# Gated feed-forward of six batches in pairs by seven block products instead of eight

## The chip, the cores and the metric

The kernel runs on one core of one Trainium2 chip. The metric is the device time of one launch in microseconds (us). Before the change three runs took 706.78, 707.29 and 708.10 us; their median is 707.29 us. The profile is one more execution, which took 706.64 us, of which 704.8 us lie between its first and its last instruction (its span).

## What is computed

Attention of 8 batches and 8 heads whose queries are pooled in twos (1152 keys, 576 pooled queries, 64 values a head), and then a feed-forward layer with a capacity: a gate scores the 576 rows of each batch, the 128 best go through two layers, and their rows are updated. All of it is float32.

```python
q_pool = q.reshape(B, H, S // 2, 2, D).mean(axis=3)
attn   = softmax(q_pool @ k.T / sqrt(D)); x = attn @ v            # (B, 576, 512) when the heads are put side by side
scores = x @ w_gate
for b in range(B):
    top = argpartition(-scores[b], 128)[:128]
    h   = maximum(x[b, top] @ w1, 0)                              # w1 512 x 1024
    ye  = h @ w2                                                  # w2 1024 x 512
    out[b, top] = x[b, top] + sigmoid(scores[b, top])[:, None] * ye
```

## The kernel before

The instructions of each engine are in the order in which the Python code records them (`manual_schedule`), and every engine works through its own list in that order. An engine waits where an operand isn't ready.

**Halves.** The work is cut by batch and pair of heads (32 pairs), and each pair into two halves of 288 pooled queries. `run` (L1307) goes through 64 halves, h = 0 to 63, four pairs and so eight halves to a batch. In the text S(h) is the start of the scores of half h on TensorE. One turn of the loop records, in this order:

- `scores(h)` (L807): nine times four matmuls into a PSUM tile of two banks, each emptied by a ScalarE exponential (`p`, L825);
- small ScalarE work for the sums: in even halves `side_by_side` (`groups`, L887), in odd ones `spread` (`sums`, L902), which reads `total`;
- `units(mid=True)`: pieces of the routing and of the feed-forward that are marked "mid";
- `gated(h-3)`, `folded(h)` (POOL adds p blocks to `acc`, L857; VectorE reduces `p` and `acc` to `fold`, L862, and then `sum`, L872), `multiplied(h-2)` (`prod`, POOL, L925), and in even halves `prepare_pair` (POOL `qp`, VectorE `kT` and `qT`);
- `weighted(h-1)` (L827): 36 matmuls with the values, the ScalarE copy `two` (L844) and the POOL addition `av` (L846); then `drained(h-1)` (VectorE `avb`, L915);
- in even halves `added` (VectorE `total`, L893), in odd ones `normalized` (VectorE `rec`, L954, and POOL `x`, L956);
- `units(mid=False)`: the pieces that are not marked "mid".

So on TensorE the mid pieces of half h stand between the scores of h and the weighting of h-1; on ScalarE they stand ahead of `two` of h-1, and so ahead of the exponentials of h+1; on VectorE the pieces at the end of h stand behind `avb` of h-1 and `total`, ahead of `folded(h+1)`.

**PSUM.** All TensorE results go through one pool, `psum`, of four tiles of two banks (`banks`, L994), used in turn. The fourth tile of `scores(h+2)` is the one that `weighted(h)` filled, and is free when `two` has copied it.

**Routing.** When a batch's gate scores are there, `routed` (L997) is a generator. Its pieces rank the rows (VectorE, L1083 to L1102), broadcast rank and gate through DRAM (`row_rank`, `lines`), pick out the 128 rows (`pick`, VectorE, L1166), make the row index (POOL, L1175), fetch the rows with an indirect DMA (POOL, L1183), transpose them (L1197), and do the first layer (L1208, 32 matmuls of 128x128 by 128) and the second (L1221, 8 of 128x128 by 512). The first layer of a batch is one mid piece, the second another. The second layer of batch 5 and both layers of batches 6 and 7 come behind the loop, where `pieces` calls in `run` interleave them by hand with the ranking of the last batch.

**The end.** The last batch's route is a chain: `acc`, `prod`, `av`, `x` on POOL; `red`, `part`, `line`, `diag` on VectorE; L1054 on TensorE; ranks on VectorE from L1092 to `pick` L1143; L1152 on TensorE; the index copied by ScalarE (L1159); the fetch by POOL (L1183); transposes (L1197); two layers; L1230; the write.

**Transfers.** Keys, queries and values of a pair come by SP's DMA queue: `load_pair` records keys and queries of pair n+2 in the second half of pair n, and `load_values` there too. Buffers: keys 2, queries 2, values 3.

## Time and profile before

| what | value |
|---|---|
| profiled execution, device time | 706.64 us |
| its span | 704.8 us |
| TensorE busy | 694.4 us (99%) |
| VectorE, ScalarE, POOL busy | 496.5, 444.5, 485.1 us |
| scores, L818 | 295.2 us |
| weighting, L836 | 294.6 us |
| first layers, L1208 | 59.3 us |
| second layers, L1221 | 57.3 us |
| DMA | 82.86 MB, 118 GB/s mean |

In the groups of the profile each line is: source line, engine, operation, written tile <- read tiles, shapes, count; then busy time, mean duration of one in ns, and idle time of the engine ahead of it with what ended it. The timeline's columns are start, length, engine, line, operation, tiles, shape and count, and in brackets idle time just before it with what ended it. A float32 matmul shows as two TensorE records, so 32 matmuls are "x64".

### The profile page before, as it was taken

The page shows a single profiled execution, that of the slowest core. Times are in us where ns is not written, and L with a number is a line of the kernel's source. Part 1 is how long each engine was busy: PE and PEld are TensorE (multiplying, and loading weights), DVE is VectorE, ACT ScalarE, POOL GpSimd, SP SyncE. Part 2 cuts the span into 40 slices and gives each one's busy share as a digit, 9 for nine tenths or more (in the row PEclk, how much of TensorE's full clock was granted, in tenths as well). Part 3 has the DMA queues.
Part 4 walks back from the last instruction along what each step waited for, and adds up shares of the span by engine and source line. Part 5 has one row for each costly group of instructions (what it writes and reads, how often), then busy time and mean ns, then how long its engine had stood idle before and what let it go on. Part 6 is the DMA issues. An engine that isn't in the chain of part 4 may idle for free.

```text
span 704.8 us, 23397 instructions
## 1 busy us (share of the span) xinstructions
PE 694.4 (99%) x9948; PEld 516.8 (73%) x9948; DVE 496.5 (70%) x793; ACT 444.5 (63%) x963; POOL 485.1 (69%) x452
## 2 busy tenths in 40 slices
PE   8999999999999999999999999999999999999996
PEld 5668899996758866688656887578775787766573
DVE  3877777996559965498754988559774697689540
ACT  6677778777547775477746776467754777477210
POOL 5877777868658695586955779467874877686520
PEclk9999999999999999999999999999999999999999
DMA  8888887858486483756928468382775728432200
GB/s 175 172 178 180 171 166 137 146 116 161 85 149 111 85 162 75 145 97 111 172 40 159 81 129 160 66 148 61 161 130 85 135 56 169 83 72 62 45 31 35
DMA packets 389490, 82.86 MB, mean 118 GB/s; under 512 B 376640, under 2 KB 376640, under 8 KB 389376
## 3 DMA queue, kind: packets, MB, share of 16 engines
q1 hardware_dynamic: 387872, 76.49, 58.1%
q0 software_dynamic: 1280, 4.20, 1.8%
q8 instruction: 80, 1.31, 0.8%
q10 hardware_dynamic: 224, 0.59, 0.3%
q14 instruction: 34, 0.28, 0.1%
HBM read 69.65 MB, written 11.59 MB: 115 GB/s over the span
## 4 chain that ended last, share of the span: by engine, by line
PE 89%; POOL 5%; issue 2%; DMA 1%; ACT 1%; DVE 1%; SPq 0%; POOLq 0%; DVEq 0%; ACTq 0%
PE ps L836 36%; PE ps L818 36%; PE ps L1208 8%; PE ps L1221 7%; POOL acc L857 2%; ACT p L825 1%; DMA kb<-in_k_dram 1%; DMA xe<-out_dram,index 1%; PE ps L1197 1%; POOL prod L925 1%; POOL x L956 0%; POOL av L846 0%; DVE fold L862 0%; POOL index L1175 0%; SPq L759 0%
## 5 line engine op out<-in xcount | busy, mean ns | idle before, releaser
L825 ACT ACTIVATE p<-ps 128x576 f32<-128x576 f32 x576 | 320.2, 695 | 1.7 <-PE ps L818 1.3
L818 PE MATMUL ps<-qT,kT 64*64 64x288 f32 x4608 | 295.2, 404 | 0.2 <-ACT p L825 0.2
L836 PE MATMUL ps<-p,v_sb 64*64 64x288 f32 x4608 | 294.6, 403 | 0.0
L857 POOL TENSOR_TENSOR acc<-p 128x576 f32<-128x576 f32 x192 | 266.3, 1417 | 15.4 <-ACT p L825 15.1
L836 PEld LDWEIGHTS ps<-p,v_sb 64*64 64x64 f32 x4608 | 215.5, 133 | 65.3 <-ACT p L825 9.2
L818 PEld LDWEIGHTS ps<-qT,kT 64*64 64x64 f32 x4608 | 208.0, 132 | 73.0 <-ACT p L825 15.4
L862 DVE TRANSPOSE_TENSOR_REDUCE fold<-p 128x54 f32<-128x1728 f32 x64 | 126.0, 1969 | 50.2 <-ACT p L825 50.2
L862 DVE TRANSPOSE_TENSOR_REDUCE fold<-acc 128x54 f32<-128x1728 f32 x64 | 125.3, 1957 | 46.0 <-POOL acc L857 45.8
L844 ACT COPY two<-ps 128x576 f32<-128x576 f32 x64 | 40.9, 639 | 156.9 <-PE ps L836 143.8
L846 POOL TENSOR_TENSOR av<-two 128x288 f32<-128x288 f32 x64 | 51.2, 800 | 96.5 <-ACT two L844 94.9
L915 DVE STREAM_TRANSPOSE avb<-av 128x288 f32<-128x288 f32 x64 | 29.4, 460 | 66.5 <-POOL av L846 66.5
L956 POOL TENSOR_TENSOR x<-avb,rec 128x576 f32<-128x576 f32 x32 | 37.1, 1159 | 40.3 <-DVE rec L954 27.9
L1208 PEld LDWEIGHTS ps<-xeT,w 128*128 128x128 f32 x512 | 57.8, 192 | 2.7 <-ACT p L825 2.6
L1208 PE MATMUL ps<-xeT,w 128*128 128x128 f32 x512 | 59.3, 277 | 0.0
L1221 PE MATMUL ps<-w,hT 128*128 128x512 f32 x128 | 57.3, 598 | 0.0
L925 POOL TENSOR_TENSOR prod<-avb,w_gate 128x288 f32<-128x288 f32 x64 | 51.5, 805 | 0.6 <-DVE avb L915 0.6
L902 ACT ACTIVATE sums<-total,tiny 32x18 f32<-32x18 f32 x124 | 38.1, 308 | 15.9 <-DVE total L893 14.2
L732 POOL TENSOR_TENSOR qp<-qb 128x576 f32<-128x576 f32 x31 | 43.8, 1414 | 2.2 <-DMA qb<-in_q_dram 2.2
L1221 PEld LDWEIGHTS ps<-w,hT 128*128 128x128 f32 x128 | 23.6, 190 | 28.1 <-issue 25.8
L735 DVE STREAM_TRANSPOSE kT<-kb 128x1152 f32<-128x1152 f32 x31 | 42.5, 1370 | 0.0
L887 ACT COPY groups<-sum 32x36 f32<-32x36 f32 x124 | 27.1, 219 | 6.7 <-DVE sum L872 5.2
L981 DVE TENSOR_TENSOR part<-red,rec 128x18 f32<-128x18 f32 x32 | 27.0, 845 | 1.1
(95 smaller groups left out, 290.6 us busy)
## 6 DMA issues: line engine op xcount, KB each, us to landing
kb<-in_k_dram SPq DMA_DIRECT2D x124, 144.0 KB
qb<-in_q_dram SPq DMA_DIRECT2D x124, 144.0 KB
v_sb<-in_v_dram SPq DMA_DIRECT2D x124, 144.0 KB
out_dram<-x SPq DMA_DIRECT2D x128, 72.0 KB
lines<-row_rank SPq DMA_DIRECT2D x7, 640.0 KB
w<-in_moe_w_dram SPq DMA_DIRECT2D x8, 512.0 KB
sc_row<-row SPq DMA_DIRECT2D x7, 288.0 KB
acc<-in_q_dram ACTq DMA_DIRECT2D x2, 288.0 KB
```

The costliest lines, as they stand in the source:

```text
L732: nc.gpsimd.tensor_tensor(out=qp[:, :, :], in0=pair["q"][:, :, 0, :], in1=pair["q"][:, :, 1, :], op=ALU.add)
L735: nc.vector.transpose(kT.rearrange("p (c g i) -> p c g i", c=self.NC, i=BLK), pair["k"].rearrange("p (g c) d -> p c g d", c=self.NC),)
L818: nc.tensor.matmul(sc[keys, j, 0:n], lhsT=pair["kT"][rows, c * P + keys.start : c * P + keys.stop], rhs=pair["qT"][rows, qs], start=True, ...
L825: nc.scalar.activation(p[:, c // G, c % G, :, :], sc[:, :, 0:n], AF.Exp, scale=self.scale)
L836: nc.tensor.matmul(av[j * self.D : (j + 1) * self.D, e, 0:n], lhsT=half["pair"]["v"][keys, j, c, :], rhs=half["p"][keys, c // G, c % G, j, :],
L844: nc.scalar.copy(two[:, :, :], av[:, :, 0:n])
L846: nc.gpsimd.tensor_tensor(out=half["av"][:, :], in0=two[:, 0, :], in1=two[:, 1, :], op=ALU.add)
L857: nc.gpsimd.tensor_tensor(out=acc[:, u, :], in0=units[:, 0, u, :], in1=units[:, 1, u, :], op=ALU.add)
L862: nc.vector.tensor_reduce(fold[:, a, :], of.rearrange("p u (m d) -> p (u m) d", d=BLK), AX.X, ALU.add, apply_transpose=True,)
L925: self.nc.gpsimd.tensor_tensor(out=pair["prod"][:, ns, :], in0=pair["avb"][:, ns, :], in1=self.w_gate[:, hp : hp + 1, :].broadcast_to([P, ...
L1208: nc.tensor.matmul(pv[:, f, 0:w], lhsT=self.w1[:, c, (f0 + f) * P : (f0 + f + 1) * P], rhs=xeT[:, c, 0:w], start=(c == 0), stop=(c == self ...
L1221: nc.tensor.matmul(ps[0:w, 0 : self.Dm], lhsT=hT[:, f, 0:w], rhs=self.w2[:, f, :], start=(f == 0), stop=(f == self.NFC - 1),)
```

## The change

Batches 0 and 1, 2 and 3, 4 and 5 go through the feed-forward as pairs. Their 256 rows and the weights are each cut into two by two blocks, and a layer is done by seven block products and 15 block sums (Strassen's scheme in Winograd's form) instead of eight products. In the first layer a product is 8 matmuls of 128x128 by 128, in the second 4 of 128x128 by 256. Batches 6 and 7 stay as they are (`layers`).

```diff
+    def weight_sums(self):
+        ...
+        for layer in (2, 1):
+            ...
+            for i, (to, x, y) in enumerate(((t1, b12, b11), (t2, b22, t1), (t3, b22, b12), (t4, b21, t2))):
+                nc.vector.tensor_tensor(out=to, in0=x, in1=y, op=ALU.subtract)      # 128x1024, L718
+                nc.sync.dma_start(kept[:, i, :], self.tw[:, i, :])                  # L719
+                yield
+    def load_sums(self, layer):
+        for i in range(0, 4, 2):
+            self.nc.sync.dma_start(self.tw[:, i : i + 2, :], self.tw_kept[layer][:, i : i + 2, :])   # L724
+            yield
+    def input_sums(self, a, s):
+        ...
+        for i, (to, x, y, op) in enumerate(
+            ((s1, a21, a22, add), (s2, s1, a11, subtract), (s3, a11, a21, subtract), (s4, a12, s2, subtract))
+        ):
+            self.nc.gpsimd.tensor_tensor(out=to, in0=x, in1=y, op=op)               # L1321
+            if i % 2:
+                yield i == 3
+    def seven_products(self, layer, a, s, c, rest, shape):
+        ...
+        steps = (
+            (a11, b11, c11, ()),
+            (s1, t1, c22, ()),
+            (s3, t3, c21, ()),
+            (s2, t2, u, ((u, c11), (c21, u), (u, c22), (c22, c21))),
+            (s4, b22, c12, ((c12, u),)),
+            (a12, b21, x, ((c11, x),)),
+            (a22, t4, y, ((c21, y),)),
+        )
+        copies = []
+        for i, (of, by, to, _) in enumerate(steps):
+            if i % 2 == 0:
+                tile = self.banks()
+            ...
+                    nc.tensor.matmul(                                               # L1355
+                        args[0], lhsT=args[1], rhs=args[2], start=k == 0, stop=k == n - 1
+                    )
+            ...
+            if i % 2 or last:
+                for copy in copies:
+                    nc.scalar.copy(*copy)                                           # L1363
+                copies = []
+            yield last
+        for *_, sums in steps:
+            for to, of in sums:
+                nc.vector.tensor_tensor(out=to, in0=to, in1=of, op=ALU.add)         # L1368
+    def layers_of_two(self, tokens):
+        ...
+        yield from self.seven_products(1, a, s, c, rest, lines)
+        loads = self.load_sums(2)
+        next(loads)
+        yield "mid"
+        for i, tile in enumerate(hidden):
+            nc.scalar.activation(tile[:, :, 0:w], tile[:, :, 0:w], AF.Relu)         # 128x1024, L1395
+            yield True if i else "mid"
+        for _ in loads:
+            pass
+        room, s = self.room_of_sums(self.NFC // 2, w)
+        for last in self.input_sums(c, s):
+            yield "hidden" if last else True
+        ...
+        yield from self.seven_products(2, quarters(hidden, self.NFC // 2), s, c, rest, lambda bank: bank[0:w, 0:half])
+        yield "mid"
+        for i, of in enumerate(c):
+            nc.scalar.activation(of, of, AF.Copy, scale=tokens[i // 2]["gate"][0:w, 0:1])   # 128x256, L1411
+        yield True
+        for i, of in enumerate(c):
+            ...
+            nc.gpsimd.tensor_tensor(out=to, in0=of, in1=to, op=ALU.add)             # 128x256, L1416
+            if i % 2:
+                self.written(token)
+                yield True
+        if tokens[1]["b"] + 1 < self.paired:
+            for _ in self.load_sums(1):
+                yield True
-                nc.gpsimd.tensor_scalar(
+                nc.vector.tensor_scalar(
                     out=index[0:w, :],
...
+                if b < self.B - 2:
+
+                    yield True
...
-        qb = self.load.tile([P, self.QB, 2, BLK], F32, name="qb")
+        qb = self.load.tile([P, self.QB, 2, BLK], F32, name="qb", bufs=1)
-        v_sb = pair["v"] = self.load.tile([P, 2, self.NC, self.D], F32, name="v_sb", bufs=3)
+        v_sb = pair["v"] = self.load.tile([P, 2, self.NC, self.D], F32, name="v_sb", bufs=2)
...
-                        self.load_values(loaded)
+                    if n + 1 < len(pairs):
+                        self.load_values(upcoming)
...
+                if h > 10 and s == 1:
+                    next(sums, None)
```

Other edits make room: several small tiles get fewer buffers (`prod` 1, `fold`, `groups`, `line` 2), `cmp`, `tie`, `flags` share the tile `pick`, the last batch's `diag` and fetched rows share `lines`, the first pair is loaded into a `p` tile, and `slot_f` is gone (`token_line` is used for it). The `pieces` calls behind the loop have other counts.

**Where it stands in the engines' lists** (from the built program; line numbers of the changed kernel):

- TensorE: the seven first-layer products of a pair are one block of 56 matmuls, between the scores of half 28 and the weighting of half 27 (and again at 44 and 60). The seven second-layer products are a block of 28 matmuls in halves 32 and 48; those of the third pair stand behind the loop. Behind the loop TensorE has: transposes of batch 6, the `sum` matmul (L967), products 1 to 3, the `diag` matmul (L1083), product 4, the `sc_row` columns (L679), products 5 to 7, 12 of the 32 first-layer matmuls of batch 6, the `pick` matmuls (L1181), the other 20, the transposes of batch 7, the rest.
- VectorE: the seven additions L1368 stand at the end of halves 28, 44, 60 behind `avb` and `total`, in half 60 behind six ranking instructions too; and at the end of halves 32 and 48 behind `avb`, `total`, the two `pick` instructions L1195 and the index L1204. In the tail they stand behind `pick` (L1172).
- ScalarE: in halves 29, 45, 61 the list is nine exponentials, four `sums`, **ReLU L1395**, `two`, nine exponentials. The second ReLU stands in the same place one half later. In halves 33 and 49 it is nine exponentials, four `sums`, **four L1411**, `two`, nine exponentials. In the tail L1411 stands ahead of the copy of the last batch's index (L1188).
- POOL: two of the hidden rows' sums (128x512) stand ahead of `acc` and two behind `x` in the halves before the second-layer block; for the third pair that is ahead of `acc` of half 63, and behind `x`, ahead of `prod` and `av` of the last half.
- SP: the sums' stores stand behind each pair's stores, their loads between the routing's transfers and the next pair's keys.

## Prediction

> **What bounds the kernel now.** I read the page's engine shares and chain first, then TensorE's timeline, then ScalarE's, VectorE's and POOL's in the same stretch, then the tail. From the page:

> ```profile
> PE 694.4 (99%) x9948; PEld 516.8 (73%) x9948; DVE 496.5 (70%) x793; ACT 444.5 (63%) x963; POOL 485.1 (69%) x452
> ...
> PE 89%; POOL 5%; issue 2%; DMA 1%; ACT 1%; DVE 1%; SPq 0%; POOLq 0%; DVEq 0%; ACTq 0%
> ```

> TensorE is busy nearly always and makes 89% of the chain of waits, so a matmul less is time less, as long as nothing makes it wait. TensorE's timeline gives the prices:

> ```profile
> 605.64 7.41 PE L1208 MATMUL ps<-xeT,w 128*128 128x128 f32 x64
> 612.99 4.59 PE L836 MATMUL ps<-p,v_sb 64*64 64x288 f32 x72
> 617.40 4.54 PE L818 MATMUL ps<-qT,kT 64*64 64x288 f32 x72
> 621.77 4.54 PE L836 MATMUL ps<-p,v_sb 64*64 64x288 f32 x72
> 626.13 4.54 PE L818 MATMUL ps<-qT,kT 64*64 64x288 f32 x72
> ```

> From start to start a first layer holds TensorE 7.35 us and half 60 8.73 us. A second layer, 535.36 to 542.42, holds it 7.06. How much ScalarE may be late is in its own timeline of half 60 (S = 617.40):

> ```profile
> 617.70 0.64 ACT L844 COPY two<-ps 128x576 f32<-128x576 f32 x1 [4.01 <-PE ps L836]
> 618.24 5.00 ACT L825 ACTIVATE p<-ps 128x576 f32<-128x576 f32 x9
> ```

> `two` starts at S+0.3, the exponentials at S+0.84, one each 0.556 us. The weighting at S+4.37 takes the PSUM tile of the sixth exponential, done at 0.84 + 6 x 0.556 = S+4.18: 0.2 us ahead. So **ScalarE has 0.2 us to spare; whatever makes `two` later than that stops TensorE.** Ahead of `two` it stands some 1.9 us a half (1.91 in half 62, by its timeline).

> The third thing is a wait inside VectorE. The same 128x128 `tie`, once beside POOL's `acc`, once beside no POOL addition:

> ```profile
> 622.06 0.92 DVE L1102 SCALAR_TENSOR_TENSOR tie<-sc_row,gate_sc,before 128x128 f32<-128x128 f32 x1
> ...
> 671.25 0.34 DVE L1102 SCALAR_TENSOR_TENSOR tie<-sc_row,gate_sc,before 128x128 f32<-128x128 f32 x1
> ```
> ```profile
> 621.42 4.19 POOL L857 TENSOR_TENSOR acc<-p 128x576 f32<-128x576 f32 x3
> ```

> The first of these three `acc` ends at 622.82; the `tie` begun at 622.06 ends at 622.98. It stood until POOL's instruction was over. By source line `tie` has a median of 619 and a maximum of 1575 ns, the latter over a second `acc`.

> [...]

> **TensorE, added and removed.** Before, the loop has six first layers and five second layers: 6 x 7.34 + 5 x 7.06 = 79.3 us. After, a first-layer block is 56 matmuls, 112 records at 7.34/64 = 0.1147: 12.85 us. A record of 256 columns isn't in the trace; the line through 0.1147 (128) and 0.4412 (512) gives 0.2236 (bounds 0.221, half of 512, and 0.230, as weight loads already overlap at 128). 56 x 0.2236 = 12.5 us. In the loop: 3 x 12.85 + 2 x 12.5 = 63.6, so -15.8. The tail gets the third pair's second layer, 12.5, for batch 5's, 5.40 + 1.81: +5.3. Net **-10.5 us**.

> **Off the path.** Eight weight sums of 1.22 us fall on VectorE between `avb` (S+2.2) and the reduction of `p` (S+5.9), where it waits anyway: nothing, at most 8 x 0.5 us if POOL's `acc` behind them sets the pace. ScalarE's product copies lie in the blocks, where it has no exponentials. POOL loses two index steps of 0.92 a pair to VectorE (0.15 each there) and its four final additions of 0.7 stand for two of 1.28; the fetch comes half a half-time later, well ahead of its transposes: nothing. The smaller pools make no wait that I find: the one `prod` buffer is read by `red` early in a half, ahead of POOL's next `prod`, which stands behind three `acc`. The sums' DMAs add 8 x 0.5 + 10 x 1.05 = 14.7 MB; at 76.5 MB in 58.1% of the span (187 GB/s) that is 79 us of the idle 40%: nothing. On SP each store of a sum waits for VectorE at about S+3.7, and behind it stand only keys that are read 17 us later; a load waits for the block to end, with the routing's and the next pair's transfers behind it, at a time when TensorE is 12 us longer in a half: nothing. One query buffer makes SP wait for POOL's `qp` of the half before, some 10 us later than now, with about 6 us left before it is read; values wait on the same release as before and have 21 us less their 10.

> **Wait A, the first ReLU (halves 29, 45, 61).** The seven additions can't start before `avb` and `total`, since the block lies ahead of the weighting whose result `avb` turns: S+2.5. POOL's `acc` wants to start at S+3.27. The first two additions pass; the first `acc` then runs 3.8 to 5.2; each further addition waits for one POOL instruction of 1.41 (or `prod`, 0.8) and makes POOL wait 0.6 in turn: third done 5.85, fourth 7.85, fifth 9.85, sixth 11.25. The ReLU needs the sixth (c11). ScalarE has been free since 7.1 (5.84, then `sums` 1.27) and stands. ReLU 11.3 to 12.3, `two` at 12.3 in place of 9.03: 3.3 late, less 0.2: **3.1 us**. In half 61 six ranking instructions with two `tie` stand ahead of the additions: **3.5**. Sum 9.7 (bounds: 0, if nothing is held up and the sixth is done at 6.4; 11).

> **Wait B, the four scalings (33, 49).** Two `pick` of 0.86, two-input too, come first, then seven additions of 0.36: against three `acc` and `prod` the sixth is done at 11.1. Four scalings at 0.35 follow; `two` starts at 12.5, 3.5 late: **3.3 each, 6.6** (bounds 0 and 7.2).

> **Wait C, second-layer sums.** After A, VectorE and POOL are some 6 us behind; POOL's third sum lands at about S+10 of halves 32 and 48, product 3 wants it at S+7.95. Bounds 0 and 2.4; part is caught up in the longer halves, I take **1.0 each, 2.0**.

> **Tail.** Lines of before:

> ```profile
> 650.72 4.12 POOL L857 TENSOR_TENSOR acc<-p 128x576 f32<-128x576 f32 x3
> ...
> 664.28 1.21 PE L1054 MATMUL ps<-diag,ones 128*128 128x288 f32 x4 [0.35 <-DVE rank_parts L1076]
> ```
> ```profile
> 676.83 1.05 POOL L1183 DMA_INDIRECT xe<-out_dram,index  x1 [5.14 <-ACT own_gate L1160]
> ...
> 680.68 0.60 PE L1197 MATMUL ps<-ident,xe 128*128 128x128 f32 x4
> ```

> The `diag` matmul already waits on the chain from the last `acc`. POOL gets two sums of 1.28 ahead of that `acc` and two ahead of the last `prod`, 5.1 us, and comes some 2 late from half 61: `acc` ends 4.8 later, `diag` some 7.3 later, TensorE's filler ahead of it being unchanged at 5.4: **+6.9** (bounds 3.7 without the lag, 7.4). The last index copy stands behind the four scalings, and those behind seven additions (0.40 each, POOL idle), 2.6 us after it could go; for batch 6 the fetch began at 649.57 and the transposes, which waited 0.61 for it, at 653.20, so a fetch takes 3.63 and this one was there at 680.46 of 680.68, 0.2 to spare; and the transposes wait **2.1** (bounds 0, 2.6).

> **Sum.** -10.5 + 9.7 + 6.6 + 2.0 + 6.9 + 2.1 = +16.8 us on a span of 704.8: 721.6. The profiled execution took 1.84 beyond its span, 706.64, 0.65 under the median of the runs; I add the difference to the median: 707.29 + 16.8 = **724.1**. With all low ends that aren't other cases (A 8.4, B 4, C 0, tail 3.7, index 1.5) 714.4; with the high ends 729.8.

> **Rivals.** (1) *Faster*: the additions aren't held up by POOL, as VectorE takes them in one go: A, B, C are nothing, the tail 3.7 + 2.1: -4.7, **702.6**. It turns at the point where the ReLU is over by S+9. For it: POOL idles 15.4 us at `acc`, waiting for ScalarE; against it: every `tie` that met an `acc`. (2) *A alone*: `pick` and scalings find room, POOL isn't late: -10.5 + 9.7 + 3.7 + 2.1 = +5.0, **712.3**. (3) *Transfers*: 2.1 MB of weight sums take 11.2 us on queues that then owe keys and values; if values lose 11 rather than their margin of 7, TensorE stands 4 us at each of five loads: **744**, on top. Against it: the DMA share falls to 2 or 3 tenths at times.

> **How the numbers follow.** The range should hold the time 8 times in 10. My forecast 0.62; (1) 0.15; (2) 0.18; (3) 0.05. Leaving out (1) and (3): 708 to 730. A measurement tells 0.2% from no change, 705.9 to 708.7: (1) lies below but for its edge, faster 0.14; same 0.04; slower 0.82.

> **What would show it.** Right: L1355 near 3 x 12.85 and 3 x 12.5 us; ScalarE waiting on L1368 ahead of L1395 and L1411; scores of halves 30, 46, 62 and 34, 50 at 7 to 8 us instead of 4.4; L1368 (128x512) near 1.3 us mean instead of 0.7; TensorE idle ahead of L967, L1083 and L1232. Wrong: L1368 at 0.7 us, or scores at 4.5 throughout.

## The result, and the profile after

| | device time, median | against before |
|---|---|---|
| before | 707.03 us (705.41 to 708.1) | |
| after | 744.62 us (743.88 to 747.49) | 1.0544, 95% interval 1.0517 to 1.0571 |

The kernel became 5.4% slower, some 38 us. The forecast was 724.1, slower by 2.4%: the sign was right, and the size too small by about 20 us. The span went from 704.8 to 742.3 us. The engines' line of the page after:

```profile
PE 694.0 (93%) x9972; PEld 515.3 (69%) x9972; DVE 554.2 (75%) x849; ACT 462.3 (62%) x1005; POOL 516.4 (70%) x474
```

TensorE's share fell from 99% to 93%. Its busy time is what it was (694.4 us before), so the added 37.5 us of span are idle time of TensorE. The saving of the blocks doesn't show in it, partly because the scores are now busy for 303.4 us instead of 295.2. VectorE got 57.7 us more to do, POOL 31.3, ScalarE 17.8. The waits of TensorE say where; the columns are who waits for whom, us in total, times, longest:

```profile
PE ps L847 <- ACT two L873: 12.5, 6, 3.1
PE ps L847 <- ACT xeT L1235: 8.4, 6, 2.0
PE ps L1232 <- DMA xe<-out_dram,index: 4.0, 2, 2.4
PE ps L1083 <- DVE rank_parts L1105: 3.7, 1, 3.7
PE ps L847 <- DVE qT L768: 3.4, 4, 1.1
PE ps L1355 <- POOL s L1321: 2.5, 2, 1.3
```

L847 are the scores, L1232 the transposes of the fetched rows, L1083 the `diag` matmul. In the profile before, the waits of TensorE on `two` and `xeT` have no line at all, and the two others that it has, on the fetch and on the ranks, were 0.6 and 0.4 us. `two`, the sums of POOL (L1321) and the ranks were foreseen. `xeT`, the fetch and `qT` (VectorE's transpose of the pooled queries) were not.

From the starts of TensorE's groups one gets what each half lasts beyond the 4.365 us of undisturbed scores or weighting. I call this the excess. Up to the end of the last weighting the loop takes 679.7 us instead of 658.0, and the tail 62.6 instead of 46.8.

| place (after) | excess, us | forecast |
|---|---|---|
| scores of halves 30, 46, 62 (wait A) | 2.4, 2.4, 5.2 | 9.7 in all |
| scores of halves 34, 50 (wait B) | 3.0, 3.0 | 6.6 in all |
| second-layer blocks (wait C), 13.86 and 13.71 us against 12.28 without the wait | 1.6, 1.4 | 2.0 in all |
| tail, +15.8 us | | 5.3 + 6.9 + 2.1 |
| halves 19 to 28: transposes of batches 0 and 1, and the scores in between and behind | 12.4 | nothing |
| halves 34 to 36, 50 to 52 (without B), 44 and 60: the same for the later batches | 5.3, 4.0, 1.0, 1.2 | nothing |

A first-layer block takes 12.70 us, where 12.85 was worked out. The 5.2 us of half 62 and the 5.3 of halves 34 to 36 each hold some 1.7 us that are no wait: behind the wait the granted clock of TensorE is 0.50 for 3.41 us (the last section shows one of them). The same happens in the tail behind the wait for the ranks. An estimate from these three stretches is 5 us of the 38.

**Wait A as it looks.** ScalarE's timeline in half 29 (S = 284.95):

```profile
290.81 1.27 ACT L931 ACTIVATE sums<-total,tiny 32x18 f32<-32x18 f32 x4
295.58 1.06 ACT L1395 ACTIVATE hT<-hT 128x1024 f32<-128x1024 f32 x1 [3.51 <-DVE hT L1368]
296.55 0.62 ACT L873 COPY two<-ps 128x576 f32<-128x576 f32 x1
```

The first ReLU stands 3.51 us for the additions L1368 and `two` comes at S+11.6. VectorE and POOL beside it:

```profile
287.49 0.67 DVE L1368 TENSOR_TENSOR s<-s,hT 128x512 f32<-128x512 f32 x1
288.19 1.92 DVE L1368 TENSOR_TENSOR hT<-hT,s 128x512 f32<-128x512 f32 x1
290.14 1.78 DVE L1368 TENSOR_TENSOR s<-s,hT 128x512 f32<-128x512 f32 x1
291.96 1.78 DVE L1368 TENSOR_TENSOR hT<-hT 128x512 f32<-128x512 f32 x1
```
```profile
288.15 5.05 POOL L886 TENSOR_TENSOR acc<-p 128x576 f32<-128x576 f32 x3 [1.38 <-ACT p L854]
```

The first addition is alone and takes 0.67 us. Each of the next three starts beside an `acc` and takes 1.78 to 1.92. The three `acc` take 5.05 instead of 4.1. This is the alternation that the prediction worked out from `tie`; that POOL is held up in turn was an assumption of the author's there, and is measured here. The prediction's lengths of instructions that the kernel before doesn't have were the author's estimates. Here the ReLU takes 1.06 us (1.0 in the prediction), a scaling L1411 0.40 from start to start (0.35), a 128x256 addition that nothing holds up 0.34 to 0.40 (0.36 and 0.40).

**What was not foreseen.** First the kernel before: VectorE's reduction of `p` in half 13, which has no routing (S = 118.28), and the same place in half 17 (S = 153.23), where the two `pick` stand ahead of it; then POOL beside these:

```profile
124.20 1.98 DVE L862 TRANSPOSE_TENSOR_REDUCE fold<-p 128x54 f32<-128x1728 f32 x1 [1.39 <-ACT p L825]
...
159.01 0.86 DVE L1166 SCALAR_TENSOR_TENSOR pick<-lines,token,token_line 128x640 f32<-128x640 f32 x1
...
161.09 1.97 DVE L862 TRANSPOSE_TENSOR_REDUCE fold<-p 128x54 f32<-128x1728 f32 x1
```
```profile
159.97 0.92 POOL L1175 TENSOR_SCALAR index<-found_token 128x1 int32<-128x1 f32 x1 [2.96 <-DVE pick L1166]
```

In half 13 the reduction comes at S+5.9 after an idle 1.39 us: that is the hole of the prediction. In half 17 it comes at S+7.9 with no idle time ahead of it. In the kernel after, VectorE in halves 17 and 18 (S(17) = 153.47, S(18) = 162.20), POOL, TensorE and ScalarE behind it:

```profile
160.91 1.40 DVE L1195 SCALAR_TENSOR_TENSOR pick<-lines,token,token_line 128x640 f32<-128x640 f32 x1
...
162.35 1.90 DVE L1195 SCALAR_TENSOR_TENSOR pick<-lines,token 128x640 f32<-128x640 f32 x1
...
164.19 0.14 DVE L1204 TENSOR_SCALAR index<-found_token 128x1 int32<-128x1 f32 x1
164.25 1.74 DVE L718 TENSOR_TENSOR tw<-w,tw 128x1024 f32<-128x1024 f32 x1
165.92 0.44 DVE L1008 TENSOR_REDUCE red<-prod 128x9 f32<-128x288 f32 x1
166.28 1.96 DVE L891 TRANSPOSE_TENSOR_REDUCE fold<-p 128x54 f32<-128x1728 f32 x1
...
170.78 0.23 DVE L983 RECIPROCAL rec<-sums 128x18 f32<-128x18 f32 x1
```
```profile
171.09 1.16 POOL L985 TENSOR_TENSOR x<-avb,rec 128x576 f32<-128x576 f32 x1 [4.43 <-DVE rec L983]
172.43 1.28 POOL L1218 DMA_INDIRECT xe<-out_dram,index  x1 [0.18 <-DVE part L1010]
173.74 4.12 POOL L886 TENSOR_TENSOR acc<-p 128x576 f32<-128x576 f32 x3
```
```profile
177.94 0.63 PE L1232 MATMUL ps<-ident,xe 128*128 128x128 f32 x4 [2.37 <-DMA xe<-out_dram,index]
...
185.56 3.92 PE L847 MATMUL ps<-qT,kT 64*64 64x288 f32 x56 [1.50 <-ACT xeT L1235]
```
```profile
182.88 1.27 ACT L931 ACTIVATE sums<-total,tiny 32x18 f32<-32x18 f32 x4 [6.04 <-DVE total L922]
184.18 0.85 ACT L916 COPY groups<-line 32x18 f32<-32x18 f32 x4
184.94 0.57 ACT L1235 COPY xeT<-ps 128x512 f32<-128x512 f32 x1
```

Read it downwards. The weight sum L718 begins where the index ended, with no idle time on either side: behind it `red`, `fold`, `sum`, `avb` and `rec` follow without a gap, so its 1.7 us pass to `rec`. POOL's `x` waits 4.43 us for `rec`, the fetch stands behind `x`, `acc` behind the fetch. The rows come late (TensorE waits 2.37), `acc` comes late, and with it `fold`, `sum`, `kT`, `qT`, `avb` and `total`. `sums` on ScalarE waits 6.04 us for `total`, and the copy `xeT` stands behind `sums`. Two causes meet here, the weight sum and the place of the fetch, and the trace alone can't divide them.

The place of the fetch acts on VectorE too. In the kernel before, POOL stood 2.96 us for `pick` ahead of the index and the fetch, and so ran no addition beside the two `pick`: 0.86 and 0.89 us. With the fetch a piece later nothing on POOL waits for `pick`; here `acc` and `prod` (158.85 to 164.92, by POOL's timeline) run beside them, and they take 1.40 and 1.90. The fourteen `pick` take 12.2 us in the kernel before, and 20.0 to 20.6 us with the fetch late (after, x3, x9, x18). With the fetch early and the index made by VectorE, the two of a batch in x8 take 0.89 us each.

### The profile page after: what moved, and what is told of

It is laid out like the page before. It is cut to its first block, busy times and chain, and to the rows that moved or that the text cites. A ratio compares the mean times of both kernels' runs of the same rounds, so it can differ in the third digit from the quotient of the medians.

```text
span 742.3 us, 23629 instructions
## 1 busy us (share of the span) xinstructions
PE 694.0 (93%) x9972; PEld 515.3 (69%) x9972; DVE 554.2 (75%) x849; ACT 462.3 (62%) x1005; POOL 516.4 (70%) x474
## 5 line engine op out<-in xcount | busy, mean ns | idle before, releaser
L847 PE MATMUL ps<-qT,kT 64*64 64x288 f32 x4608 | 303.4, 410 | 24.3 <-ACT two L873 12.5
L886 POOL TENSOR_TENSOR acc<-p 128x576 f32<-128x576 f32 x192 | 274.7, 1459 | 19.5 <-ACT p L854 19.2
L847 PEld LDWEIGHTS ps<-qT,kT 64*64 64x64 f32 x4608 | 199.5, 134 | 114.9 <-ACT p L854 28.4
L865 PEld LDWEIGHTS ps<-p,v_sb 64*64 64x64 f32 x4608 | 213.0, 133 | 66.7 <-ACT p L854 11.6
L875 POOL TENSOR_TENSOR av<-two 128x288 f32<-128x288 f32 x64 | 53.1, 830 | 75.0 <-ACT two L873 70.4
L954 POOL TENSOR_TENSOR prod<-avb,w_gate 128x288 f32<-128x288 f32 x64 | 56.3, 879 | 0.6 <-DVE avb L944 0.6
L1008 DVE TENSOR_REDUCE red<-prod 128x9 f32<-128x288 f32 x64 | 27.5, 430 | 0.4 <-POOL prod L954 0.4
L1121 DVE TENSOR_SCALAR_CACHE_REDUCE pick<-sc_row,gate_sc 128x576 f32<-128x576 f32 (+4 forms) x40 | 21.6, 539 | 5.6 <-ACT gate_sc L682 5.4
L1363 ACT COPY hT<-ps 128x512 f32<-128x512 f32 (+1 forms) x15 | 7.9, 545 | 27.5 <-PE ps L1355 22.7
L1363 ACT COPY s<-ps 128x256 f32<-128x256 f32 (+1 forms) x27 | 11.5, 447 | 21.4 <-PE ps L1355 21.4
```

The lines of the kernel that those rows point to most:

```text
L847: nc.tensor.matmul(sc[keys, j, 0:n], lhsT=pair["kT"][rows, c * P + keys.start : c * P + keys.stop], rhs=pair["qT"][rows, qs], start=True, ...
L865: nc.tensor.matmul(av[j * self.D : (j + 1) * self.D, e, 0:n], lhsT=half["pair"]["v"][keys, j, c, :], rhs=half["p"][keys, c // G, c % G, j, :],
L875: nc.gpsimd.tensor_tensor(out=half["av"][:, :], in0=two[:, 0, :], in1=two[:, 1, :], op=ALU.add)
L886: nc.gpsimd.tensor_tensor(out=acc[:, u, :], in0=units[:, 0, u, :], in1=units[:, 1, u, :], op=ALU.add)
L954: self.nc.gpsimd.tensor_tensor(out=pair["prod"][:, ns, :], in0=pair["avb"][:, ns, :], in1=self.w_gate[:, hp : hp + 1, :].broadcast_to([P, ...
```

## The experiments

After seeing the trace I took the later fetch for the cause of nearly all the missing 20 us: in the kernel before, the fetch was issued in an even half, ahead of `acc` but not behind `x`, and the transposes fell into even halves, where ScalarE has no `sums` ahead of `xeT`. The rivals were VectorE's added instructions wherever the fetch stands, SP's queue, and the smaller pools. In the table, ratios are to the kernel before on the same chip; a point below is 1% of the time before, 7.07 us.

| run | what | median us | ratio (95%) |
|---|---|---|---|
| x1_fetch_early | after, fetch early | 742.62 | 1.0495 (1.0474 to 1.0515) |
| x2_before_fetch_late | before, fetch late | 727.04 | 1.0278 (1.0256 to 1.0299) |
| x3_no_additions | after without additions | 721.12 | 1.0193 (1.0164 to 1.0221) |
| x4_weights_copied | after, sums replaced by copies | 734.92 | 1.0379 (1.0356 to 1.0403) |
| x5_early_copied | x1 and x4 | 737.56 | 1.0413 (1.0394 to 1.0432) |
| x6_early_no_additions | x1 and x3 | 714.72 | 1.0113 (1.0078 to 1.0147) |
| x7_late_neither | x3 and x4 | 715.55 | 1.0106 (1.0055 to 1.0157) |
| x8_early_neither | x1, x3 and x4 | 713.30 | 1.0075 (1.0045 to 1.0105) |
| x9_one_input | additions with one input | 736.29 | 1.0396 (1.0332 to 1.0460) |
| x10_behind_two | ReLU, scalings behind `two` | 743.25 | 1.0531 (1.0468 to 1.0594) |
| x11_no_stores | weight sums not stored | 746.27 | 1.0544 (1.0495 to 1.0593) |
| x12_two_groups | batches 4, 5 plain | 737.60 | 1.0423 (1.0386 to 1.0460) |
| x13_before_pools | before, pools of after | 706.80 | 1.0000 (0.9989 to 1.0011) |
| x14_sums_sooner | weight sums in halves 10 to 17 | 741.86 | 1.0491 (1.0463 to 1.0519) |
| x15_two_groups_early | x1, x12 and x14 | 731.37 | 1.0352 (1.0317 to 1.0387) |
| x16_clean_floor | fetch early, no sums or additions | 707.24 | 1.0002 (0.9986 to 1.0019) |
| x17_late_floor | fetch late, no sums or additions | 709.00 | 1.0051 (1.0028 to 1.0073) |
| x18_no_weight_sums | after without weight sums | 734.93 | 1.0409 (1.0388 to 1.0430) |

### The place of the fetch: x1, x2, x16, x17

```diff
 x1
-                if b < self.B - 2:
-
-                    yield True
...
 # layers_of_two: the blocks stay in their halves
+        yield True
         yield True
         a = quarters([token["xeT"] for token in tokens], self.ND // 2)
```

> The changed kernel with the fetch of the rows back at the end of the even half in which the index is made, and with the transposes back in even halves; one piece of delay is put behind the second batch's transposes instead, so that both block products stay in their places. Theory (the later fetch puts the copy of the fetched rows behind the sums that wait for VectorE's total, and the fetch itself behind POOL's x): the waits of TensorE for xeT and for the fetched rows, about 18 us in all, shrink to the 3 to 4 us that the kernel before has, and the time falls from 744.6 to about 728 us. Rival (VectorE's added instructions make everything late wherever the fetch stands): 738 to 745 us, with the same waits in the halves next door.

It fell by 0.5 points (interval 0.15 to 0.83), not 2.3. My theory as stated fell with it. TensorE no longer waits for `xeT`, but 17.8 us for `two` and 5.9 for fetched rows: in half 26 the rows are late all the same, and in halves 34 and 50 the transposes now share ScalarE's queue with the four scalings (excess 5.9 and 5.6, against 3.0 for the scalings alone).

x2 is the kernel before with `nc.vector` for the index and the same extra `yield True`.

> The kernel before with one part of the change alone: the index of the rows by VectorE and the fetch one piece later, so that the transposes of batches 0 to 5 fall into odd halves. If the later fetch costs by itself, all six transposes pay: 707 plus 8 to 15 us, 715 to 722 us. If it costs only together with VectorE's added instructions (weight sums, additions): 707 to 711 us. If the place of the fetch is nothing: 706 to 708 us.

In the kernel before, the same move costs 20 us (2.8%), above the highest expectation. There it also moves the plain layers from one half to the next. TensorE's waits have 9.6 us for `xeT`, six times, as expected; the scores of halves 26, 34, 42, 50 and 58 are 1.2 us late each as well. VectorE's two `pick` take 1.41 and 1.90 us beside POOL's `acc` in five of the six batches, and in one the first takes 4.28:

```profile
248.67 4.28 DVE L1166 SCALAR_TENSOR_TENSOR pick<-lines,token,token_line 128x640 f32<-128x640 f32 x1
```

This is 11.3 us more of VectorE's time over six batches; how much of the 20 us follows from it no run tells. So this number can't be carried over to the kernel after.

x16 and x17 take the rest away: no additions, no weight sums and no stores, plain weights loaded instead, with the fetch early and late.

```diff
-                nc.vector.tensor_tensor(out=to, in0=x, in1=y, op=ALU.subtract)
-                nc.sync.dma_start(kept[:, i, :], self.tw[:, i, :])
-                yield
+                pass
+        yield from self.load_sums(1)
...
-            self.nc.sync.dma_start(self.tw[:, i : i + 2, :], self.tw_kept[layer][:, i : i + 2, :])
+            of = self.w1_in.rearrange("(c p) f -> p c f", p=P)
+            self.nc.sync.dma_start(self.tw[:, i : i + 2, :], of[:, i : i + 2, :])
...
-        for *_, sums in steps:
-            for to, of in sums:
-                nc.vector.tensor_tensor(out=to, in0=to, in1=of, op=ALU.add)
```

> Fetch early, no additions, and no weight sums or stores or copies: plain weights are loaded from the inputs in place of the sums (another output). What is left is the block products with their copies, POOL's sums, the loads and the pools. If the copies by DMA cost the 6 us of half 26 in x8_early_neither: 713.3 minus 5 to 7, 706 to 708 us. If the pools or the added copies on ScalarE cost it: 711 to 714 us.

> As x16_clean_floor (no additions, no weight sums, plain weights loaded from the inputs; another output), but with the fetch late as in the changed kernel. Against 707.2 with the fetch early: 709 to 714 us if the late fetch costs by itself 2 to 6 us, as the pairs of runs so far have it; 720 us or more if it costs as much as the later fetch did in the kernel before (20 us); 706 to 708 us if it is nothing.

The floor is the time of before, 1.0002: even with no additions and no weight sums the block products bring nothing. Its loop ends at 647.4, 10.6 us sooner; its tail takes 59.1, 12.3 longer. Against it the late fetch costs 0.49 points, 3.5 us, give or take 2.0. x17's waits show `xeT` again, and no wait for rows:

```profile
PE ps L844 <- ACT xeT L1232: 6.5, 5, 2.0
```

### The additions: x3, x9, x10

x3 leaves out the last three lines of the diff above and nothing else.

> The changed kernel with the seven additions behind each block product left out, so that the products are not put together and the output is another. Theory: the waits behind the first ReLU and behind the four scalings go (10.0 and 6.0 us in the trace), the rest stays but for 1 to 3 us in the halves just behind: 725 to 729 us. If the additions also make the later halves' copies late, 720 us or less. If something else held the ReLU, above 735 us.

3.5 points, some 25 us: more than A and B, and next to the case that the additions also make the halves behind late. A and B are gone, 16.0 us. The second-layer blocks fall to 12.28 each, 3.0 us: wait C came from the additions too. The tail loses 3.2, of which 2.1 lie ahead of the last index copy (the 20 first-layer matmuls of batch 6 with the wait behind them: 6.66 us with the additions, 4.57 without). The rest is net of the halves behind: 34 to 36 fall from an excess of 5.3 (without B) to 2.2, but 44 grows from 1.0 to 4.1.

```diff
 x9
-                nc.vector.tensor_tensor(out=to, in0=to, in1=of, op=ALU.add)
+                nc.vector.tensor_scalar(
+                    out=to, in0=of, scalar1=0.0, scalar2=None, op0=ALU.add, op1=ALU.add,
+                    accum_out=self.spare[0 : to.shape[0], :],
+                )
```

> The seven additions behind each block product become seven one-input instructions of the same size (x plus zero, with an accumulator, so that the products are not put together and the output is another). Theory[...] (a two-input addition of VectorE and POOL's acc hold each other up): with one input each takes about 0.55 us instead of 1.0 to 1.4 for 512 columns, the seven end 3 to 5 us earlier, and most of the waits behind the first ReLU and the scalings go: 731 to 736 us. Rival (seven more instructions in VectorE's queue cost that much by themselves[...]): 742 to 745 us.

With one input each:

```profile
L1369 DVE TENSOR_SCALAR_CACHE_REDUCE hT<-s 128x512 f32<-128x512 f32 x12 | 8.2, 686 | 1.2
```

686 ns on average instead of 1029 to 1417, with the same `acc` on POOL. The scores of halves 30 and 46 wait no more, those of 34 and 50 0.8 us. The time falls by 1.5 points (10 us). So the second input beside POOL carries about 10 of the 25 us (the interval is 5 us to either side): with two inputs these additions took 1.78 to 1.92 us beside `acc`, with one 0.69. The other 15 remain with seven short instructions: half 62 keeps 4.1 us, halves 36 and 52 about 4, and the tail all of its 63 us. The mean granted clock of this profile is 0.985, against 0.992 in the kernel after, so part of what remains is lowered clock; how much, and in which halves, is not shown.

x10 replaces `yield "mid"` ahead of the first ReLU and of the scalings by `yield True`.

> The changed kernel with the first ReLU and the four scalings moved behind the copy of the weighting's results to SBUF (two) of their half, instead of ahead of it; the output is the reference's. Theory (they wait for additions and hold the copy, and with it TensorE): half a half later, 4.4 us, most of the additions are done: waits of 10.0 and 6.0 us shrink to 2 to 5 in all, 731 to 735 us. Rival (ScalarE then waits in the next place and holds the exponentials instead): 740 to 745 us.

The rival holds: no change that can be told from none. TensorE's first wait is now another:

```profile
PE ps L847 <- ACT p L854: 12.2, 5, 3.1
```

against 12.5 us for `two` before the move. The ReLU waits less (5.7 us instead of 11.8), but it stands ahead of the exponentials instead, and halves 30, 46 and 50 lose 2.5, 3.8 and 4.3 us (at a mean granted clock of 0.987 in this profile, 0.992 before the move). With 0.2 us to spare on ScalarE, the order on it doesn't help when its input is late.

### The weight sums: x4, x11, x14, x18

x4 replaces each `tensor_tensor` and store by a DMA of a plain quarter into the store, for the first layer also into `tw`; x18 is the clean form, with the loads of the diff above and the additions kept.

> The changed kernel with VectorE's eight sums of weight quarters left out: plain quarters are copied by DMA into the room of the sums and into the store instead, so that the output is another. Theory (the place of the fetch decides): only the stretch of halves 11 to 26 can gain, some 2 to 4 us of its waits: 740 to 743 us. Rival (the weight sums make the early transposes wait): the waits of halves 19 to 28, about 11 us, go: 733 to 735 us.

> The changed kernel with its weight sums and their stores left out and plain weights loaded from the inputs in their place (another output); additions and late fetch stay. If the eight sums cost what x4_weights_copied says: 733 to 736 us. If the copies there cost something too: 729 to 733 us.

Both take off 1.4 to 1.7 points, 10 to 12 us. In x18 the excess of halves 19 to 28 falls from 12.4 to 2.0 us. VectorE and POOL of x18 in the stretch shown above:

```profile
164.11 0.14 DVE L1201 TENSOR_SCALAR index<-found_token 128x1 int32<-128x1 f32 x1
164.18 0.44 DVE L1005 TENSOR_REDUCE red<-prod 128x9 f32<-128x288 f32 x1
...
169.04 0.22 DVE L980 RECIPROCAL rec<-sums 128x18 f32<-128x18 f32 x1
```
```profile
169.34 1.16 POOL L982 TENSOR_TENSOR x<-avb,rec 128x576 f32<-128x576 f32 x1 [3.60 <-DVE rec L980]
```

Counted from the start of the index, `rec` comes 1.66 us sooner and `x` 1.67, nearly the weight sum's own 1.74. The transposes of this batch (L1229) then start without a wait.

> VectorE's eight weight sums stay, but their eight stores of 512 KB to DRAM are left out, and the later loads read plain weights of the same size (another output). Theory (the sums cost by VectorE's time): 742 to 745 us, the early waits of halves 19 to 28 as before. Rival (SyncE waits for each sum before its store, and behind it stand the loads of the next half and the ranks of the routing, so that the queue and not VectorE makes the fetch late): 733 to 737 us, as where the sums were left out.

Without the stores the ratio is 1.0544, that of the changed kernel, within 0.5 points. The stores on SP's queue are not the cause.

> The changed kernel with its eight weight sums in halves 10 to 17, one in each, instead of in the odd halves 11 to 25; the output is the reference's. If they cost by the halves in which they stand (next to the transposes and the ranks of batches 0 and 1), most of the 9.7 us comes back: 735 to 739 us. If they cost VectorE's time wherever they stand, 742 to 746 us.

x14 issues one sum in each half from 10 (`if h > 9` for `if h > 10 and s == 1`). It brings 0.5 points, little of what was hoped. Halves 24 to 28 fall from an excess of 7.7 to 1.3 us, but halves 16 to 20 now have 8.8 instead of 4.7. The two changes nearly cancel, so the sums cost about as much in these halves as in the others.

### Pairs of these: x5, x6, x7, x8

> Fetch early as in x1_fetch_early, and weight quarters copied by DMA in place of VectorE's eight sums as in x4_weights_copied (another output); the additions stay. If the early fetch gained little in x1_fetch_early because the weight sums made the index late as well, it gains here in halves 19 to 28, where 3 us of waits are left, and in halves 36 and 52 as before: 734.9 minus 3 to 7, 728 to 732 us. If its little gain had another reason (the transposes in even halves meet the four scalings in halves 34 and 50), 732 to 735 us.

> Fetch early, and the seven additions behind each block product left out (another output); the weight sums stay. The meeting of transposes and scalings in halves 34 and 50 costs nothing without additions, so the early fetch should gain more here than the 2 us of x1_fetch_early: 721.1 minus 5 to 9, 712 to 716 us. If the place of the fetch is of no account, 719 to 721 us.

> Fetch late as in the changed kernel, with neither weight sums nor additions (another output). If the two losses simply add, 744.6 minus 23.5 minus 9.7: 711 us. If they share waits, more than that is left: 713 to 716 us.

> Fetch early, with neither weight sums nor additions (another output): what is left of the change is the block products with their copies, POOL's sums, the loads and the smaller pools. If the place of the fetch is a loss of its own, hidden in x1_fetch_early by the other two, this falls to 698 to 703 us, below the kernel before by most of the 10.5 us of saved matmuls; if weight sums and additions are all that costs, 708 to 711 us, the same as the late fetch.

x6 says that without additions the early fetch is worth 0.8 points, x1 that with them it is worth 0.5. x5 and x8 came out above both of their ranges. x5, x7 and x8 hold copies by DMA in place of the weight sums, and x8 shows in VectorE's timeline what these do: `pick` stands 4.43 us for `lines` ahead of 238.07. The broadcast of the ranks stands on SP's queue behind two of my 512 KB copies, and half 26 loses 6.2 us (3.9 in its scores, 2.3 in the weighting behind its transposes). That is the experiment's own cost, and half 26 of x5 has it too. x7 lies 0.55 points above its clean form x17, just about its interval. So x16 to x18 were made without copies, and x5, x7 and x8 decide nothing.

### Pools, and the third group: x13, x12, x15

x13 is the kernel before with `bufs` and `load_values` as in the kernel after.

> The kernel before with the changed kernel's pools alone: one buffer of queries, two of values (loaded one pair later), one of prod, and fewer of the small tiles; the output is the reference's. If the smaller pools are nothing, as the prediction had it: 706 to 708 us. If SyncE's wait for the single buffer of queries (76 us in the changed kernel's trace) makes ranks, keys and fetches late, 710 to 717 us.

1.0000: the smaller pools cost nothing.

x12 sets `self.paired = self.B - 4 - self.B % 2` and takes the `pieces` calls and the place of `units` in the last turn from the kernel before. x15 adds the edits of x1 and x14.

> Block products for batches 0 to 3 only; batches 4 and 5 have the plain two layers, and the end of the kernel has the order of the kernel before. The output is the reference's. What the third group costs, from the trace of the changed kernel: 15.8 us in the tail (62.6 after the last weighting against 46.8) and 5.1 behind its ReLU, against 3.9 us that its blocks save in the loop before that. 744.6 minus 15.8 minus 5.1 plus 9.0 (plain layers of batches 4 and 5 in the loop 21.7 for 12.7): 732 to 734 us. If the end of the kernel is late for another reason (the smaller pools), the tail stays above 55 us and the time above 740.

> What the runs point to, put together: block products for batches 0 to 3 only, the fetch early, the weight sums in halves 10 to 17; the output is the reference's. Batches 4 and 5 then stand as in the kernel before. From 737.6 (two groups): minus 8 to 13 for the fetch (six transposes and the plain layers back in their places), minus 4 to 7 for the sums: 718 to 726 us. If the early fetch returns no more than the 2 us that it did in the changed kernel, 729 to 733 us.

The tail shrinks to 49.0 and 47.8 us, so it is the third group that makes it long. But x12's loop gets longer than that of the changed kernel by 7.6 us (687.3), where 3.9 were expected (9.0 for plain layers less 5.1 behind the ReLU). Its scores show late halves as x2's do: 1.2 us in half 58, 1.6 in 60. x15, the fastest that still computes the whole result, is 3.5% slower than the kernel before. No version that beats the kernel before came out of these runs.

## Why the prediction was wrong

The kernels with a late fetch build the change up from the floor, in points of 707 us:

| step | ratio | us | forecast |
|---|---|---|---|
| block products, copies, POOL's sums, tail (x16) | 1.0002 | +0.1 | -10.5 + 6.9 = -3.6 |
| fetch a piece later (x17) | 1.0051 | +3.5 | nothing |
| weight sums (x3) | 1.0193 | +10.0 | nothing, at most 4 |
| additions (after) | 1.0544 | +24.8 | 9.7 + 6.6 + 2.0 + 2.1 = 20.4 |

Each difference is known to 1 to 3 us. Taken in the other order the additions cost 25.3 (x18 less x17) and the weight sums 9.5; with the fetch early they cost 27.0 (x1 less x6) and 7.8 (x6 less x16). So the shares hardly depend on the order, and they make up the whole 38 us. Of the 21.6 us by which the forecast missed (38.4 less 16.8), the weight sums are 10.0, the additions 4.4, the block products and their tail 3.7, and the fetch 3.5.

- **The step that failed most**: "Eight weight sums of 1.22 us fall on VectorE between `avb` (S+2.2) and the reduction of `p` (S+5.9), where it waits anyway: nothing, at most 8 x 0.5 us". The 1.22 was the author's estimate, and the shortest of the eight took 1.21. They took 1.73 and 1.96 us on average by form (up to 3.15), as two-input instructions beside POOL's additions, and VectorE wasn't waiting there: with `red`, ranks or `pick` in its queue, the reduction of `p` of half 17 started without a gap at S+7.9 even before the change, and after it at S+12.8. Cost 10 us, nearly half of what was missed. The hole was taken from halves without routing, and the added time was priced without the hold-up by POOL that the same text used for the additions. POOL pays as well: the `av` beside the weight sum shown takes 1.78 us, by POOL's timeline, where one alone takes 0.80. How the 10 us divide between the sums' own length and the hold-up was not tested.
- **"The fetch comes half a half-time later, well ahead of its transposes: nothing"** failed in three ways. Behind `x`, which waits for `rec`, the fetch comes as late as VectorE is. And the transposes changed their parity: in odd halves ScalarE has `sums` ahead of `xeT`, and these wait for `total`. And POOL no longer stands still while VectorE runs `pick`, which takes 3.3 us there instead of 1.75. The text looked at the time until the transposes and not at the queues that the step was moved past, nor at what its wait had kept apart. Cost 3.5 us here; no run divides the three.
- **A, B, C and the index copy** were right in mechanism: 10.0, 6.0, 3.0 and 2.1 in the trace for 9.7, 6.6, 2.0 and 2.1. That A comes so near is in part luck: 1.7 of its 10.0 us are lowered clock in half 62, which the prediction did not have. x3 bears out the additions, x9 the second input. The remaining 4 us of the additions are what comes behind: after B, the same lateness holds `xeT` two halves later.
- **TensorE** has its blocks at 12.70 and 12.28 us (12.85 and 12.5 forecast). The loop of the floor gains 10.6 of 15.8: the prediction took the whole saving of the matmuls for a saving of time, and small waits of scores take part of it back (1.7 in half 20, 1.1 in 28, 2.2 in 44). Another 1.7 is a slower start in that one profile.
- **The tail** grew by 15.8 us for 14.3 forecast, by 12.3 in the floor. Its waits after, in TensorE's timeline:

```profile
682.75 0.38 PE L967 MATMUL ps<-sum,merge 128*128 128x36 f32 x2 [2.15 <-DVE sum L901]
...
692.10 2.13 PE L1083 MATMUL ps<-lines,ones 128*128 128x288 f32 x4 [3.71 <-DVE rank_parts L1105]
...
713.79 0.63 PE L1232 MATMUL ps<-ident,lines 128*128 128x128 f32 x4 [1.93 <-DMA lines<-out_dram,index]
```

- **Pools, stores and transfers** at nothing were right (x13, x11). Rival 3 reached 744 us, but by transfers; no wait of TensorE for values or keys came with it. It was the right time for a wrong reason.
- What stays open: how the 20 us that the move of the fetch costs in the kernel before divide between the longer `pick`, the waits for `xeT` and the moved plain layers, and how the last 15 us of the additions divide between VectorE's queue and what stands behind it.

## What to carry to other kernels

An engine that is 70% busy, as VectorE was in the kernel before, may still have no hole where you want to put something: look in the timeline of the very halves in which the new instruction will stand, and if it starts and ends without idle time on either side, its whole length goes down the chain (1.66 of the weight sum's 1.74 us did here). Price every added instruction by the same contention as the one that you worry about. When a step is moved by one place in a list, ask on each engine what will stand ahead of it there, not only how much time it has left, and what its wait had kept from running beside something else.

## What the runs showed of the hardware

A wait of TensorE cost more than itself in x1. TensorE stood 3.15 us ahead of the transposes of half 26, which begin at 248.04. A window just behind (start and end, length, PE busy and records, granted clock, DMA share, GB/s):

```profile
249.00:251.00 2.00, 2.00 (x17) 0.50 0.91 241
```

The granted clock was 0.50 for some 6 us behind the wait, and the weighting there took 6.8 us instead of 4.4: another 2.4 lost, three quarters of the wait again.

Clock 0.50 stood behind shorter waits too, at times. Scores of halves 36 and 52 in the kernel after, each behind the same wait for `xeT`, and stretches within them in the same columns as above:

```profile
370.90 5.32 PE L847 MATMUL ps<-qT,kT 64*64 64x288 f32 x56 [1.99 <-ACT xeT L1235]
...
550.80 3.92 PE L847 MATMUL ps<-qT,kT 64*64 64x288 f32 x56 [2.00 <-ACT xeT L1235]
```
```profile
371.50:374.50 3.00, 3.00 (x32) 0.50 1.13 231
551.00:554.00 3.00, 3.00 (x48) 1.00 1.07 249
```

A wait of 1.99 us was followed by clock 0.50, one of 2.00 was not, nor were those of halves 34 and 50 with 2.44. So the length of the single wait doesn't decide it; what does, no run here shows.
